# Where a batch's loads stand among the DMA transposes: k and v apart from q, tied in between the u transposes

## The chip, the cores and the metric

The kernel runs on one core of one Trainium2 chip. The metric is the device time of one execution in microseconds (us). PE is TensorE (PEld its weight loads), DVE is VectorE, ACT is ScalarE, POOL is GpSimd, and SP is the queue that issues plain DMA stores and DMA transposes. An *eviction* is a copy of a finished product out of the memory banks that PE writes to; PE can reuse the bank after it. The *granted clock* is the share of full speed at which TensorE was clocked. A kernel's span in its profile is about 2 us shorter than its time.

## The reference, cut to what matters

Linformer attention for 8 batches of 8 heads, then an MLP mixer on each batch:

```python
k_proj = einsum('ks,bhsd->bhkd', E, k)          # k and v: [8, 8, 1024, 64] f32, E and F: [64, 1024]
v_proj = einsum('ks,bhsd->bhkd', F, v)
attn   = softmax(q @ k_proj^T / 8)              # 64 keys
x      = attn @ v_proj                          # heads joined: [8, 1024, 512]
u      = x + (relu(x^T @ w_tok1) @ w_tok2)^T    # token mixing
out    = u + relu(u @ w_ch1) @ w_ch2            # channel mixing
```

## The kernel before

Per batch there is a *front* (k and v projections, scores, attention, token mixing, which yields `u`) and two channel-mixing *half-layers* of 512 rows each. A half-layer needs `u` transposed. SP does this by DMA: `uT0` for the even half-layer, `uT1` for the odd one. I call them the first and the second u transpose. Four additions and subtractions on VectorE, the *S sums*, are the first readers of a uT. While the half-layers of batch b run on PE, the front of batch b+1 is woven in. q is also transposed by DMA. k, v and q are loaded by GpSimd DMAs (f32 to bf16), two of half the heads for each.

The order of every engine's instructions is made before anything runs. A planner in the program gives each job a time, by priority and by the model below, and the instructions are then written down in the order of those times. Each engine's queue then keeps that order on the chip. Semaphores give the waits.

```python
LAG = {"PE": 0.25, "DVE": 0.15, "ACT": 0.15, "POOL": 0.2, "DMA": 1.0}
# every job: engine, occupancy, latency; an engine takes its jobs one after another.
# "DMA" is one such engine, for all loads, stores and transposes together.
def sp(t, fn, **kw):                 # store: t = 1.5, transpose: t = 3.5
    return pl.add("DMA", t, t + 1.0, fn, **kw)

def ld(mb, fn, **kw):                # a load of half the heads: mb = 0.262 * 4
    t = mb / 0.40
    return pl.add("DMA", t, t + 2.0, fn, **kw)

def tie(j, other):                   # j waits for other, in the plan and by a semaphore
    j.deps.add(other)
    tied[j] = other
...
def token2(b, si, due):              # u rows; after the 4th and the 8th: a u transpose
    ...
            if landed[0]:
                tie(j, landed[0])    # the u transpose behind the last-listed load
            turned[0] = j
...
def s_sums(j):                       # half-layer j
    one(0, a21, a22, add=True)       # VectorE, bf16, quarters of uT
    one(2, a11, a21)
    one(1, St[:, 0], a11, deps=(0,))
    one(3, a12, St[:, 1], deps=(1,))
...
def load_batch(b):                   # called in front(b - 1), behind attention
    jobs = [load_heads(b, n, hh, H // 2, None) for n in "kvq" for hh in range(0, H, H // 2)]
    for j in jobs if turned[0] else ():
        tie(j, turned[0])            # behind the second q transpose
    landed[0] = jobs[-1]
...
for b in range(B):
    for j in (2 * b, 2 * b + 1):
        s_sums(j)
        for m in range(SETS):
            up_set(j, m)             # PE: L801 before, L802 after
        down_block(j)                # PE: L896 before, L897 after
    if b + 1 < B:
        at = 2 * TU * (b + 1)
        if b > 0:
            q_transpose(None)
        front(b + 1, at - 62, at - 14)
```

The softmax here doesn't subtract the row's maximum and nothing guards it: scores larger than these inputs give would overflow.

Of the kernel before, what the change touches and what calls it, by code (L numbers as in the profile page):

```python
# [34 lines left out]
class Planner:  # L35
# [36 lines left out]
    def plan(self):  # L72
        for j in self.jobs:
            for d in j.deps:
                d.next.append(j)
        for j in reversed(self.jobs):
            if j.prio is None:
                due = [s.prio for s in j.next]
                j.prio = (min(due) if due else 1e9) - j.occ - 0.3
        for j in self.jobs:  # L80
            if j.prio > 1e8:
                j.prio = max((d.prio for d in j.deps), default=0) + 2
        free = {}
        waiting = {j.n: len(j.deps) for j in self.jobs}
        can = {}
        est = {}

        def open_(j):
            est[j.n] = max((d.end + self.LAG[d.eng] if d.eng != j.eng else d.full for d in j.deps), default=0.0)
            can.setdefault(j.eng, []).append(j)  # L90

        for j in self.jobs:
            if not waiting[j.n]:
                open_(j)
        bank_free = [0.0] * 8
        clean = [True] * 8
        held = dict.fromkeys(self.caps, 0)
        left = {}
        for j in self.jobs:
            for b in j.banks:  # L100
                left[id(b)] = left.get(id(b), 0) + 1
        order = []
        turn = {n: [b for j in self.jobs for b in j.takes if b.stream == n] for n in self.caps}

        def home(b, now):

            if held[b.stream] == self.caps[b.stream]:
                return None
            if b.stream in "UD" and turn[b.stream][0] is not b:
                return None  # L110
            best = None
            keep = [i for i in self.homes["U"] if clean[i] and bank_free[i] is not None]
            if all(clean[:5]):
                keep = []
            for i in self.homes[b.stream]:
                t = bank_free[i]
                if t is None or (b.seeded and not clean[i]):
                    continue
                if not b.seeded and clean[i] and keep and keep[-1] == keep[0] == i:
                    continue  # L120
                c = (max(now, t), clean[i], t, i)
                if best is None or c < best:
                    best = c
            return best

        while any(can.values()):
            pick = None
            for e, js in can.items():
                f = free.get(e, 0.0)
                cands = []  # L130
                for j in js:
                    t = max(f, est[j.n])
                    spot = None
                    if j.takes:
                        h = home(j.takes[0], t)
                        if h is None:
                            continue
                        t, spot = h[0], h[3]
                    cands.append((t, j.prio, j.n, j, spot))
                if not cands:  # L140
                    continue
                t0 = min(c[0] for c in cands) + 0.02
                c = min((c for c in cands if c[0] <= t0), key=lambda c: (c[1], c[2]))
                if pick is None or c[0] < pick[0]:
                    pick = c
            if pick is None:
                raise RuntimeError("no job can go on", [(j.eng, j.fn.__qualname__, j.prio) for js in can.values() for j in js][:20], held, bank_free)
            t, _, _, j, spot = pick
            can[j.eng].remove(j)
            j.start, j.end, j.full = t, t + j.lat, t + j.lat + 0.03  # L150
            free[j.eng] = t + j.occ
            if j.takes:
                b = j.takes[0]
                b.at = spot
                turn[b.stream].remove(b)
                held[b.stream] += 1
                bank_free[spot] = None
            for b in j.banks:
                left[id(b)] -= 1
                if not left[id(b)]:  # L160
                    held[b.stream] -= 1
                    bank_free[b.at] = max(x.end for x in b.jobs) + 0.1
                    clean[b.at] = b.full
            order.append(j)
            for s in j.next:
                waiting[s.n] -= 1
                if not waiting[s.n]:
                    open_(s)
        assert len(order) == len(self.jobs), (len(order), len(self.jobs))
        return order  # L170
# [3 lines left out]
def kernel(  # L174
# [16 lines left out]
    B, H, S, D = q.shape  # L191
# [20 lines left out]
    last = {}  # L212
# [92 lines left out]
    def sp(t, fn, **kw):  # L305
        return pl.add("DMA", t, t + 1.0, fn, **kw)
# [201 lines left out]
            writes=[("kT", 1, h) for h in heads], uses=[bk],  # L508
        )

    turned = [None]
    landed = [None]

    def q_transpose(due):
        for h in range(0, H, H // 2):
            before = turned[0]
            turned[0] = sp(
                3.5,
                lambda h=h: nc.sync.dma_start_transpose(
                    out=qT[:, h : h + H // 2].rearrange("p h j s -> p (h j) s"),  # L520
                    in_=q_sb[:, h : h + H // 2].rearrange("p h si d -> p (h si d)"),
                ),
                reads=[("q", i) for i in range(h, h + H // 2)],
                writes=[("qT", i) for i in range(h, h + H // 2)], prio=due,
            )
            if before:
                turned[0].deps.add(before)

    def q_transpose_pe(hp, due):
        bk = Bank(stream[0], full=False)  # L530
# [93 lines left out]
    def token2(b, si, due):  # L624
        bk = Bank(stream[0], full=False)

        def mm():
            for t in range(TC):
                nc.tensor.matmul(  # L629
                    bank(bk), wt2_sb[:, t, si::NSI], hT_sb[:, t, :],  # L630
                    start=(t == 0), stop=(t == TC - 1),
                )

        pe(
            TC, 512, mm, reads=["wt2"] + [("hT", t, hp) for t in range(TC) for hp in range(HP)],
            takes=[bk], prio=due,
        )
        dve(
            512,
            lambda: nc.vector.tensor_add(  # L640
                out=u_t[b % 2][:, si, :], in0=bank(bk), in1=x_sb[:, si, :]
            ),
            reads=[("x", h, si // NJ) for h in range(H)], writes=[("u", b % 2, si)], uses=[bk],
        )
        if si % NJ == NJ - 1:
            i = si // NJ
            j = sp(
                3.5,
                lambda: nc.sync.dma_start_transpose(
                    out=uT_t[i].rearrange("p s dc q -> p (s dc) q"),  # L650
                    in_=u_t[b % 2][:, i * NJ : (i + 1) * NJ].rearrange("p s d -> p (s d)"),
                ),
                reads=[("u", b % 2, n) for n in range(i * NJ, (i + 1) * NJ)],
                writes=[("uT", i, n) for n in range(HP)], prio=None,
            )
            if landed[0]:
                tie(j, landed[0])
            turned[0] = j

    def quarter(j, sh, dh):  # L660
        return uT_t[j % 2][:, 2 * sh : 2 * sh + 2, 2 * dh : 2 * dh + 2, :]
# [314 lines left out]
            u_transpose_pe(hp, i, (-5.5 if i == 0 else 1.5) + 0.5 * hp)  # L976
    stream[0] = "F"

    def load_batch(b):
        jobs = [load_heads(b, n, hh, H // 2, None) for n in "kvq" for hh in range(0, H, H // 2)]  # L980
        for j in jobs if turned[0] else ():
            tie(j, turned[0])
        landed[0] = jobs[-1]

    def front(b, begin, end):
        units = []
# [5 lines left out]
        for i in range(H // hn):  # L992
            unit(1.9 * hn / H, lambda t, i=i: kv_proj(b, i * hn, hn, t))
            unit(0.9 * hn / H, lambda t, i=i: k_transpose(i * hn, hn, t))
            if b == 1:
                for hp in range(2 * i, 2 * i + 2):
                    unit(0.4, lambda t, hp=hp: q_transpose_pe(hp, t))
        unit(0.4, lambda t: scores(0, t))
        unit(0.4, lambda t: scores(1, t))
        for h in range(H):  # L1000
            if h + 2 < H:
                unit(0.4, lambda t, h=h: scores(h + 2, t))
            for half in range(2):
                unit(0.25, lambda t, h=h, half=half: attend(h, half, t))
        if b + 1 < B:
            unit(0.0, lambda t: load_batch(b + 1))
        for n in range(TC):
            unit(1.8, lambda t, n=n: token1(n, t))
        for si in range(NSI):
# [10 lines left out]
# [4 lines that stand above are left out]
                up_set(j, m)  # L1024
            down_block(j)
        if b + 1 < B:
            at = 2 * TU * (b + 1)
            if b > 0:
                q_transpose(None)
            front(b + 1, at - 62, at - 14)  # L1030
    gate = mybir.DependencyInfo(mybir.DependencyClass.Sync, mybir.DependencyReason.DATA)
    plan = pl.plan()
# [41 lines left out]
```

## Time and profile before

| | before |
|---|---|
| time, median of the first 3 runs | 439.78 us (438.99 to 440.23) |
| PE busy | 418.5 of 439.5 us |
| VectorE waits for a u transpose, before the S sums | 1.5 us, once |
| u transpose, issue to landing | 4.3 to 7.2 us |

The page of the kernel before: its span, the busy times, the granted TensorE clock in 40 slices, and the chain of work that ended last by engine.

```profile
span 439.5 us, 9315 instructions
...
PE 418.5 (95%) x3736; PEld 338.4 (77%) x3736; DVE 321.0 (73%) x783; ACT 241.1 (55%) x439; POOL 106.2 (24%) x122
...
PEclk9999999999999999999999999999999999999999
...
PE 86%; DVE 7%; ACT 2%; DMA 2%; issue 1%; DVEq 0%; ACTq 0%
```

PE is busy nearly always and heads the chain, so a change to loads can only remove the few gaps that PE has. The waits of the kernel before (us in total, how often, the longest):

```profile
PE ps L896 <- DVE da L943: 2.7, 4, 0.9
...
DVE S L671 <- DMA uT<-u: 1.5, 1, 1.5
...
PE ps L578 <- DVE x_sb L595: 0.6, 1, 0.6
```

VectorE stood in front of an S sum once, and PE waited 0.6 us for attention's evictions (`x_sb`). Now the DMA side. First GpSimd's timeline around the loads of batch 4 (start, us, engine, line, operation, in brackets the idle time before it), then SP's around one slow u transpose, then the landing times of all transposes of that tile:

```profile
149.56 0.78 POOL L314 DMA_DIRECT2D q_sb<-in_q_dram  x1 [1.68 <-DMA qT<-q_sb]
...
154.40 1.52 POOL L314 DMA_DIRECT2D k_sb<-in_k_dram  x2
155.90 1.50 POOL L314 DMA_DIRECT2D v_sb<-in_v_dram  x2
157.36 0.78 POOL L314 DMA_DIRECT2D q_sb<-in_q_dram  x1
```

```profile
269.21 4.67 SPq L649 DMA_TRANSPOSE uT<-u  x1
...
287.62 3.09 SPq L649 DMA_TRANSPOSE uT<-u  x1
```

```profile
DMA to landing us min/median/max: 4.3/4.6/7.2
```

The loads go out in one bundle behind the q transposes and are in flight until about the next first u transpose, which beside them took up to 7.2 us (4.3 us for batch 3, when they had all but landed). From batch 2 on, the second u transpose starts 12 to 18 us after the first, when PE has read the old uT.

### The profile page before, as it was taken

How to read it: one execution, taken by the hardware profiler on the slowest of the kernel's cores; microseconds unless marked ns; L12 is line 12 of the kernel's file. 1: busy time of each engine (PE TensorE's matmuls, PEld its weight loads, DVE VectorE, ACT ScalarE, POOL GpSimd, SP SyncE). 2: the span in 40 equal slices, each digit the busy share in tenths (PEclk: the TensorE clock that was granted, in tenths of full speed). 3: DMA queues.
4: the chain of work that ended last, by engine and by line, in shares of the span. 5: the costliest groups of instructions: out<-in, count | busy, mean ns of one | idle time of the engine just before them, and what ended most of it. 6: DMA issues, size and time to landing. Idle time of an engine off the chain costs nothing.

```text
span 439.5 us, 9315 instructions
## 1 busy us (share of the span) xinstructions
PE 418.5 (95%) x3736; PEld 338.4 (77%) x3736; DVE 321.0 (73%) x783; ACT 241.1 (55%) x439; POOL 106.2 (24%) x122
## 2 busy tenths in 40 slices
PE   6789999999999999999999999899999999999993
PEld 4468888578778886788778877688768886888883
DVE  3459969678978797779697696778697596966451
ACT  1557786258536754567356654558436663555540
POOL 8442123032301331115021331115112210212212
PEclk9999999999999999999999999999999999999999
DMA  9999979289955899198955899187992811241022
GB/s 167 208 199 207 206 123 195 91 186 167 177 94 152 126 194 172 46 224 149 197 89 120 139 189 203 22 193 140 199 142 47 195 48 49 50 145 61 36 98 95
DMA packets 89516, 60.89 MB, mean 139 GB/s; under 512 B 55681, under 2 KB 84865, under 8 KB 89473
## 3 DMA queue, kind: packets, MB, share of 16 engines
q0 software_dynamic: 30624, 29.36, 42.7%
q1 hardware_dynamic: 58768, 30.68, 29.4%
q8 instruction: 29, 0.48, 0.4%
q10 hardware_dynamic: 80, 0.26, 0.3%
q14 instruction: 15, 0.11, 0.1%
HBM read 59.24 MB, written 16.78 MB: 173 GB/s over the span
## 4 chain that ended last, share of the span: by engine, by line
PE 86%; DVE 7%; ACT 2%; DMA 2%; issue 1%; DVEq 0%; ACTq 0%
PE ps L896 32%; PE ps L801 30%; PE ps L609 6%; PE ps L629 5%; PE ps L555 3%; PE ps L455 3%; PE ps L578 3%; DMA uT<-u 2%; DVE S L671 1%; DVE u L728 1%; PE ps L539 1%; ACT qT L547 1%; PE ps L377 1%; PE ps L689 1%; DVE da L943 1%
## 5 line engine op out<-in xcount | busy, mean ns | idle before, releaser
L896 PEld LDWEIGHTS <-G 128*128 128x128 bf16 x1344 | 130.0, 98 | 24.5 <-issue 5.7
L896 PE MATMUL ps<-wc_sb,G 128*128 128x256 bf16 x768 | 103.8, 273 | 3.9 <-DVE da L943 2.7
L801 PEld LDWEIGHTS <-wc_sb 128*128 128x128 bf16 x768 | 73.6, 98 | 14.3 <-issue 1.6
L823 ACT ACTIVATE G<-ps 128x512 bf16<-128x512 f32 x96 | 57.2, 599 | 39.9 <-PE ps L801 39.6
L896 PE MATMUL ps<-wT,G 128*128 128x256 bf16 x576 | 77.7, 272 | 0.1
L927 POOL TENSOR_TENSOR o<-o,u 128x512 f32<-128x512 f32 x32 | 37.4, 1169 | 130.3 <-ACT o L925 115.2
L801 PEld LDWEIGHTS <-wT 128*128 128x128 bf16 x576 | 55.1, 98 | 11.2 <-issue 2.2
L801 PE MATMUL ps<-uT,wc_sb 128*128 128x256 bf16 x384 | 57.6, 273 | 0.0
L801 PE MATMUL ps<-S,wc_sb 128*128 128x256 bf16 x384 | 57.6, 273 | 0.0
L927 POOL TENSOR_TENSOR db<-db,u 128x512 f32<-128x512 f32 x16 | 18.9, 1182 | 157.5 <-ACT db L925 157.5
L801 PE MATMUL ps<-S,wT 128*128 128x256 bf16 x384 | 54.9, 273 | 0.9 <-ACT G L823 0.7
L640 DVE TENSOR_TENSOR u<-ps,x_sb 128x512 bf16<-128x512 f32 x56 | 35.7, 684 | 22.2 <-PE ps L629 21.7
L595 DVE TENSOR_TENSOR x_sb<-ps,rdn 128x256 bf16<-128x256 f32 x128 | 49.7, 415 | 0.3
L836 DVE TENSOR_TENSOR G<-G 128x512 bf16<-128x512 bf16 x96 | 46.7, 489 | 3.4
L782 DVE CUSTOM_DVE_ANT_0 g<-ps,ub 128x512 bf16<-128x512 f32 x48 | 32.8, 684 | 20.4 <-PE ps L801 20.3
L782 DVE CUSTOM_DVE_ANT_0 G<-ps,ua 128x512 bf16<-128x512 f32 x48 | 32.7, 682 | 18.1 <-ACT ua L829 18.0
L564 ACT ACTIVATE a<-ps 128x512 bf16<-128x512 f32 x64 | 37.1, 600 | 12.4 <-PE ps L555 12.2
L829 ACT COPY ua<-ps 128x512 f32<-128x512 f32 x48 | 28.1, 586 | 24.2 <-PE ps L801 23.6
L829 ACT COPY ub<-ps 128x512 f32<-128x512 f32 x48 | 28.1, 586 | 9.6 <-PE ps L801 9.2
L842 ACT COPY ps<-ps 128x512 f32<-128x512 f32 x48 | 28.3, 589 | 6.9 <-DVE g L782 4.2
L578 PE MATMUL ps<-vb,a 128*128 128x130 bf16 x256 | 30.9, 226 | 0.6 <-DVE x_sb L595 0.6
L629 PE MATMUL ps<-hT_sb,wt_sb 128*128 128x512 bf16 x112 | 29.5, 379 | 0.0
(69 smaller groups left out, 521.7 us busy)
## 6 DMA issues: line engine op xcount, KB each, us to landing
out_dram<-o SPq DMA_DIRECT2D x32, 512.0 KB, 3.6
k_sb<-in_k_dram POOLq DMA_DIRECT2D x14, 512.0 KB, 8.6
v_sb<-in_v_dram POOLq DMA_DIRECT2D x14, 512.0 KB, 13.0
q_sb<-in_q_dram POOLq DMA_DIRECT2D x14, 512.0 KB, 9.9
wc_sb<-in_moe_w_ch_dram POOLq DMA_DIRECT2D x6, 256.0 KB, 12.9
wc_sb<-in_moe_w_ch_dram POOLq DMA_DIRECT2D x4, 384.0 KB, 12.1
k_sb<-in_k_dram POOLq DMA_DIRECT2D x4, 256.0 KB, 6.7
v_sb<-in_v_dram POOLq DMA_DIRECT2D x4, 256.0 KB, 7.2
```

The costliest lines, as they stand in the source:

```text
L564: lambda: nc.scalar.activation(out=a_t[h % 4], in_=bank(bk), func=ACT.Exp, scale=scale),
L578: nc.tensor.matmul(view()[:, 2 * jj : 2 * jj + 2].rearrange("p c d -> p (c d)"), a_t[h % 4][:, j * P : (j + 1) * P], vb[:, h].rearrange("k ...
L595: lambda: nc.vector.tensor_tensor(out=x_sb[:, 4 * half : 4 * half + 4, h * D : (h + 1) * D], in0=view()[:, :, 0:D], in1=rdn[:, :, None].to ...
L629: nc.tensor.matmul(bank(bk), wt2_sb[:, t, si::NSI], hT_sb[:, t, :], start=(t == 0), stop=(t == TC - 1),)
L640: lambda: nc.vector.tensor_add(out=u_t[b % 2][:, si, :], in0=bank(bk), in1=x_sb[:, si, :]),
L782: nc.vector._custom_dve(TENSOR_ADD_SAT, out=out, in0=in0, in1=in1, s0=FMAX, s1=0.0)
L801: nc.tensor.matmul(t[:, c, :], w1_of(n, dd, 2 * m + c), a_of(j, n, dd), start=(n in (1, 7) and c == 0 and dd == 0), stop=(c == 1 and dd == 1),
L823: lambda: nc.scalar.activation(out=G[:, n, cs], in_=view(src), func=ACT.Relu),
L829: 512, lambda: nc.scalar.copy(out=dst, in_=view("y")), writes=[(name, s % 2)],
L836: 512, lambda: f(out=G[:, n, cs], in0=in0, in1=in1), ps=False, reads=deps,
L896: nc.tensor.matmul(view(X_OF[n])[:, t, :], G[:, G_OF[n], cc, t * P : (t + 1) * P], w2_of(n, cc), start=(n in (1, 7) and t == 0 and cc == 0 ...
L927: 512, lambda: nc.gpsimd.tensor_add(out=dst, in0=dst, in1=u_of(sh, dh)),
```

## The change

The intent, as the edit reads: the loads are parted into two groups, and each is tied in between transposes, so that no transpose runs beside loads. k and v of batch b+2 go behind the k and v projections of batch b+1 and behind batch b's first u transpose, and batch b's second u transpose waits for the last of them. The q loads go behind the q transposes, and the next first u transpose waits for them. The q transposes themselves move forward, behind the second u transpose of the batch before the one they followed.

```diff
-                due = [s.prio for s in j.next]
+                due = [s.prio for s in j.next if s.prio is not None]
...
-    def q_transpose(due):
+    def q_transpose(b, behind):
...
+        landed[0] = load_group(b + 1, "q", j) if b + 1 < B else None
...
-            if landed[0]:
+            if i == 0 and landed[0]:
                 tie(j, landed[0])
-            turned[0] = j
+            turned_u[b, i] = j
...
-    def load_batch(b):
-        jobs = [load_heads(b, n, hh, H // 2, None) for n in "kvq" for hh in range(0, H, H // 2)]
-        for j in jobs if turned[0] else ():
-            tie(j, turned[0])
-        landed[0] = jobs[-1]
+    def load_group(b, names, behind):
+        jobs = [load_heads(b, n, hh, H // 2, None) for n in names for hh in range(0, H, H // 2)]
+        for j in jobs if behind else ():
+            tie(j, behind)
+        return jobs[-1]
+
+    def load_kv(b):
+        last = load_group(b, "kv", turned_u.get((b - 2, 0)))
+        if (b - 2, 1) in turned_u:
+            tie(turned_u[b - 2, 1], last)
...
+        if b + 1 < B:
+            unit(0.0, lambda t: load_kv(b + 1))       # in front(b), behind the projections
+        if b == 1:
+            unit(0.0, lambda t: load_group(2, "q", None))
...
-                q_transpose(None)
+                q_transpose(b + 1, turned_u.get((b - 1, 1)))
```

More of the change, by code (lines that the diff above doesn't have):

```diff
@@ L509, in k_transpose @@
         )
-    turned = [None]
+    turned_u = {}
     landed = [None]
-    def q_transpose(due):
+    def q_transpose(b, behind):
         for h in range(0, H, H // 2):
-            before = turned[0]
-            turned[0] = sp(
+            j = sp(
                 3.5,
@@ L523, in q_transpose @@
                 reads=[("q", i) for i in range(h, h + H // 2)],
-                writes=[("qT", i) for i in range(h, h + H // 2)], prio=due,
+                writes=[("qT", i) for i in range(h, h + H // 2)], prio=None,
             )
-            if before:
-                turned[0].deps.add(before)
+            if behind:
+                j.deps.add(behind)
+            behind = j
+        landed[0] = load_group(b + 1, "q", j) if b + 1 < B else None
     def q_transpose_pe(hp, due):
@@ L1004, in front @@
                 unit(0.25, lambda t, h=h, half=half: attend(h, half, t))
-        if b + 1 < B:
-            unit(0.0, lambda t: load_batch(b + 1))
         for n in range(TC):
```

## The prediction

> **What bounds it now.** The page gives PE 418.5 of 439.5 us (95%). The Trainium skill ("Trainium Kernel Development and Optimization", opening section) warns that matmul busy time is a bad metric because matmuls overlap, so I looked at the spacing of starts: 256-column matmuls start 0.109 us apart, and from 40 to 427 us only about 4 us are lost in gaps (0.85 us at 92, 0.71 and 0.61 at 280-283, 0.73 at 327, 0.55 at 358, 0.44 at 381). Over 2% faster (8.8 us) is not to be had.
>
> **What loads cost now.** In the DMA issues, batch b+1's six loads go out after batch b's second q transpose (q, k, k, v, v, q) and run until the u transpose: 149.6 to 174.3, 250 to 274, 300 to 326 us. The u transpose's tie is to the q half issued first, so it runs beside the others. Alone it lands in 4.3 us (173.6); beside loads it took 7.15 (269.2) and 6.54 us (321.0). This agrees with the same skill page ("Key Constraints": all queues share the 16 DMA engines). There the S sums, its readers, start on landing (276.4, 327.9), and the PE gaps at 280 and 327 follow: about 2 us in all. That is what the change can win.
>
> **What it moves.** No arithmetic, no bytes. The two q loads stay behind the q transposes; the four of k and v go between the first and second u transpose. The loads' priority no longer sees the u transpose's due, so I expect issue order k, k, v, v, and the tie on the last v makes the second u transpose wait for all four: the first lands 5.5 us after issue, others 2.55 us apart (landings 44.6 to 57.4): 13.2 us, plus 0.55 us to issue. Now the second u transpose starts 7.6 to 11.3 us after the first landed (held by PE readers of the old uT); so it moves 3 to 6 us later, and the q transposes queue behind it. For batch 1, where both u transposes go at 87 and 90 us, the second slips to about 105, and batch 2's q transposes by about 15 us.
>
> **New loop.** First u transpose (4.3) + k/v loads (13.75) + second u transpose and both q transposes (12.2, from 287.6 to 299.65) + q landing to the next u transpose (20 to 24 now; about 17 if attention is put first) = 47 to 51 us, estimated. PE's period is about 49.3 us. Five such loops follow 91.7 us, then about 103 us of work (estimated from matmul counts times 0.109): 91.7 + 5 x 49.3 + 103 = 441. So the slack in the DMA chain is spent. I expect slightly slower, near break-even.
>
> **Predicted:** 442 us, 80% range 437 to 452. Faster by 2%: 0.02; same: 0.80; slower: 0.18.
>
> **What would show it.** First u transposes all landing in 4.3 to 4.6 us, no loads beside them; second u transposes 13 us or more after that landing; batch 2's scores at about 115 instead of 101 us; the gaps near 280 gone but new ones where S sums wait for uT. PE busy stays about 418 us.
>
> **What would make it wrong.** If attention cannot be compressed below 20 us, the loop takes 51 us or more and the time reaches 450. If the last v is issued first, the second u transpose hardly moves and the time falls to 437-438. The static order of all engines is replanned, which alone can move a microsecond or two.

## The result, and the profile after

The changed kernel took 457.18 us (median of 4 runs, 455.83 to 459.05), the kernel before 440.00 (4 runs, 438.99 to 443.09). The ratio is 1.038 with a 95% interval of 1.032 to 1.045. It is slower by 3.8%, outside the predicted range. Ratios here are the mean time of one kernel's fast runs over that of the other's of the same rounds, so not quite the ratio of the medians that I quote. Executions over 1.5% slower than the fastest of the same kernel are left out of the means.

The page of the changed kernel, the lines that answer to those above:

```profile
span 455.9 us, 9334 instructions
...
PE 421.7 (92%) x3736; PEld 338.5 (74%) x3736; DVE 320.2 (70%) x783; ACT 243.3 (53%) x439; POOL 105.2 (23%) x122
...
PEclk9799999999899999998999999998999999999998
...
PE 78%; DVE 10%; DMA 7%; ACT 2%; issue 1%; DVEq 0%; ACTq 0%
```

Busy times hardly changed (PE +3.2 us), but PE's share of the chain fell from 86 to 78%, and DMA's rose from 2 to 7%. Three dips of the granted clock have appeared inside the kernel. Its waits:

```profile
DVE S L672 <- DMA uT<-u: 16.4, 6, 3.5
...
PE ps L579 <- DVE x_sb L596: 5.5, 5, 2.7
...
PE ps L802 <- DMA uT<-u: 4.6, 2, 3.6
...
PE ps L802 <- DVE x_sb L596: 2.9, 1, 2.9
```

VectorE now stands in front of S sums six times, 16.4 us in all, and PE waits for u transposes and for attention's evictions. In GpSimd's and SP's timelines around the k and v loads of batch 5:

```profile
185.91 1.15 POOL L928 TENSOR_TENSOR o<-o,u 128x512 f32<-128x512 f32 x1 [2.28 <-ACT o L926]
187.35 1.52 POOL L314 DMA_DIRECT2D k_sb<-in_k_dram  x2 [0.29 <-PE ps L458]
188.86 0.76 POOL L314 DMA_DIRECT2D v_sb<-in_v_dram  x1
194.11 1.15 POOL L928 TENSOR_TENSOR o<-o,u 128x512 f32<-128x512 f32 x1 [4.49 <-ACT o L926]
195.22 0.79 POOL L314 DMA_DIRECT2D v_sb<-in_v_dram  x1
```

```profile
177.91 1.98 SPq L650 DMA_TRANSPOSE uT<-u  x1
195.29 1.55 SPq L921 DMA_DIRECT2D out_dram<-o  x2
205.17 1.78 SPq L650 DMA_TRANSPOSE uT<-u  x1
```

The loads start 9.4 us after the first u transpose, because PE (the projection, L458) still reads the buffers. The last v goes out 7.9 us after the first k and lands at 205.12, 17.8 us after it, with two stores in flight beside it. The second u transpose starts at 205.17, which is 27.3 us after the first. In the kernel before, these gaps were 2.9 us for batch 1 and 12.1 to 18.4 us after that. What that does on VectorE and on PE, in their timelines:

```profile
206.29 0.75 DVE L596 TENSOR_TENSOR x_sb<-ps,rdn 128x256 bf16<-128x256 f32 x2
209.57 1.15 DVE L672 TENSOR_TENSOR S<-uT 128x512 bf16<-128x512 bf16 x1 [2.52 <-DMA uT<-u]
...
211.10 0.42 DVE L596 TENSOR_TENSOR x_sb<-ps,rdn 128x256 bf16<-128x256 f32 x1
```

```profile
208.43 0.28 PE L579 MATMUL ps<-vb,a 128*128 128x130 bf16 x2
211.57 1.01 PE L802 MATMUL ps<-uT,wc_sb 128*128 128x256 bf16 x4 [2.87 <-DVE x_sb L596]
```

An S sum stands at the head of VectorE's queue and its operand lands at 209.55. Attention's matmuls were done by 208.7, but the eviction that would free PE's next bank runs only at 211.1, behind the S sum. So PE stands for 2.87 us. The Trainium skill ("TensorE: Matmul & The Clock Gate", section "Architectural detail") says that ACT and DVE are strict FIFO, and this trace agrees. And PE runs at half speed just afterwards. The windows view of the changed kernel (columns: stretch, length, busy time and instructions of each engine, granted clock, DMA share, GB/s):

```profile
207.40:210.80 3.40, 1.31 (x14) 1.09 (x13) 1.23 (x3) 1.64 (x3) 1.18 (x2) 1.00 1.14 212
210.80:214.20 3.40, 2.62 (x13) 1.89 (x13) 2.78 (x10) 1.17 (x2) 0.00 (x0) 0.50 1.02 192
```

There are three such windows (118.6, 210.8 and 316.6 us), each of 3.4 us at half clock behind a PE gap of 2.7 to 3.6 us. They cost at most 3 x 1.7 = 5.1 us (half of each window). They are not the main loss: two other runs of this kernel, with a mean clock of 0.994 instead of 0.978, had room for at most one such window and still took 455.83 and 456.49 us, only 2.0 and 1.4 us less. The landing times of all transposes of that tile in the changed kernel:

```profile
DMA to landing us min/median/max: 4.2/4.5/8.9
```

The transposes did become quick, as intended: the slow one, 8.9 us, is batch 1's first, beside the first q loads.

### The profile page after: what moved, and what is told of

Read it like the earlier page. It is cut to its first block, busy times and chain, and to the rows that moved or that the text cites. A ratio compares the mean times of both kernels' runs of the same rounds, so it can differ in the third digit from the quotient of the medians.

```text
span 455.9 us, 9334 instructions
## 1 busy us (share of the span) xinstructions
PE 421.7 (92%) x3736; PEld 338.5 (74%) x3736; DVE 320.2 (70%) x783; ACT 243.3 (53%) x439; POOL 105.2 (23%) x122
## 4 chain that ended last, share of the span: by engine, by line
PE 78%; DVE 10%; DMA 7%; ACT 2%; issue 1%; DVEq 0%; ACTq 0%
PE ps L802 29%; PE ps L897 28%; DMA uT<-u 7%; PE ps L610 5%; PE ps L630 5%; PE ps L455 3%; PE ps L579 3%; PE ps L556 3%; DVE S L672 2%; DVE x_sb L596 1%; DVE G L837 1%; DVE u L729 1%; ACT qT L548 1%; PE ps L377 1%; PE ps L540 1%
## 5 line engine op out<-in xcount | busy, mean ns | idle before, releaser
L897 PEld LDWEIGHTS <-G 128*128 128x128 bf16 x1344 | 131.0, 98 | 27.8 <-issue 4.0
L897 PE MATMUL ps<-wc_sb,G 128*128 128x256 bf16 x768 | 104.9, 275 | 2.8 <-DVE da L944 1.6
L802 PE MATMUL ps<-uT,wc_sb 128*128 128x256 bf16 x384 | 58.8, 277 | 7.4 <-DMA uT<-u 4.6
L802 PE MATMUL ps<-S,wc_sb 128*128 128x256 bf16 x384 | 58.6, 276 | 0.0
L802 PE MATMUL ps<-S,wT 128*128 128x256 bf16 x384 | 56.5, 276 | 0.6 <-DVE S L672 0.6
L928 POOL TENSOR_TENSOR db<-db,u 128x512 f32<-128x512 f32 x16 | 18.4, 1152 | 158.6 <-ACT db L926 158.6
L596 DVE TENSOR_TENSOR x_sb<-ps,rdn 128x256 bf16<-128x256 f32 x128 | 50.8, 415 | 0.7
L641 DVE TENSOR_TENSOR u<-ps,x_sb 128x512 bf16<-128x512 f32 x56 | 38.0, 686 | 12.6 <-PE ps L630 12.3
L837 DVE TENSOR_TENSOR G<-G 128x512 bf16<-128x512 bf16 x96 | 43.7, 460 | 3.6 <-DVE G L837 0.5
L783 DVE CUSTOM_DVE_ANT_0 G<-ps,ua 128x512 bf16<-128x512 f32 x48 | 32.8, 684 | 15.8 <-ACT ua L830 15.2
L830 ACT COPY ua<-ps 128x512 f32<-128x512 f32 x48 | 28.1, 586 | 22.4 <-PE ps L802 21.8
L579 PE MATMUL ps<-vb,a 128*128 128x130 bf16 x256 | 31.7, 224 | 5.8 <-DVE x_sb L596 5.5
L830 ACT COPY ub<-ps 128x512 f32<-128x512 f32 x48 | 28.1, 586 | 14.6 <-PE ps L802 14.6
L843 ACT COPY ps<-ps 128x512 f32<-128x512 f32 x48 | 27.9, 580 | 14.9 <-PE ps L802 13.6
L630 PE MATMUL ps<-hT_sb,wt_sb 128*128 128x512 bf16 x112 | 32.7, 381 | 0.0
```

Of the source, the lines that this page charges most:

```text
L579: nc.tensor.matmul(view()[:, 2 * jj : 2 * jj + 2].rearrange("p c d -> p (c d)"), a_t[h % 4][:, j * P : (j + 1) * P], vb[:, h].rearrange("k ...
L596: lambda: nc.vector.tensor_tensor(out=x_sb[:, 4 * half : 4 * half + 4, h * D : (h + 1) * D], in0=view()[:, :, 0:D], in1=rdn[:, :, None].to ...
L630: nc.tensor.matmul(bank(bk), wt2_sb[:, t, si::NSI], hT_sb[:, t, :], start=(t == 0), stop=(t == TC - 1),)
L641: lambda: nc.vector.tensor_add(out=u_t[b % 2][:, si, :], in0=bank(bk), in1=x_sb[:, si, :]),
L783: nc.vector._custom_dve(TENSOR_ADD_SAT, out=out, in0=in0, in1=in1, s0=FMAX, s1=0.0)
L802: nc.tensor.matmul(t[:, c, :], w1_of(n, dd, 2 * m + c), a_of(j, n, dd), start=(n in (1, 7) and c == 0 and dd == 0), stop=(c == 1 and dd == 1),
```

## The experiments

*Waits* below is the total of VectorE's waits for a u transpose before S sums, over the whole span. *Last v* is the time from the first issue to the landing of the last of batch 5's four loads. *uT1* is the time from the start of batch 3's first u transpose to the landing of its second. Times are medians of the fast runs; waits, last v and uT1 are from one profiled run each. Ratio is against the kernel before in the same rounds. The row of the kernel before gives its first three runs. Its medians in the three later sessions were 439.8 to 440.1 us.

| kernel | time, us | ratio (95%) | waits | last v | uT1 |
|---|---|---|---|---|---|
| before | 439.8 | 1 | 1.5 | (other place) | 17.7 |
| changed | 457.2 | 1.038 (1.032 to 1.045) | 16.4 | 17.8 | 31.6 |
| e1_no_wait | 449.3 | 1.020 (1.013 to 1.028) | 9.8 | 18.4 | 30.5 |
| e2_burst | 457.1 | 1.039 (1.034 to 1.044) | 16.3 | 18.1 | 32.0 |
| e3_untied | 452.5 | 1.028 (1.024 to 1.032) | 13.0 | 14.3 | 24.4 |
| e4_first | 458.4 | 1.040 (1.033 to 1.046) | 16.7 | 15.8 | 27.8 |
| e5_small_stores | 459.0 | 1.043 (1.037 to 1.049) | 17.6 | 17.7 | 31.6 |
| e6_small_loads | 440.2 | 1.003 (0.999 to 1.006) | 1.6 | 13.3 | 28.1 |
| e7_honest_plan | 440.0 | 1.001 (0.999 to 1.004) | 4.2 | 17.8 | 31.7 |
| e8_early_kv | 454.3 | 1.033 (1.027 to 1.038) | 8.8 | 14.4 | 26.2 |
| e9_small_stores_all | 446.6 | 1.015 (1.011 to 1.018) | 7.6 | 15.6 | 29.5 |
| e10_sums_later | 453.0 | 1.030 (1.026 to 1.035) | 13.0 | 17.4 | 31.3 |
| e11_plan_half | 442.8 | 1.006 (1.003 to 1.009) | 7.4 | 16.8 | 30.7 |
| e12_best | 437.4 | 0.994 (0.991 to 0.996) | 2.0 | 17.8 | 31.8 |

### First round: is it the wait?

My first theory (A) was that the semaphore wait of the second u transpose on the last v costs the time. Rivals: the replanned order as such (B), and competition on the DMA engines (C). In e1 every engine's order is exactly that of the changed kernel (compared instruction by instruction), and only the wait is gone.

```diff
-            tie(turned_u[b - 2, 1], last)
+            turned_u[b - 2, 1].deps.add(last)        # e1: in the plan only
```

> The changed kernel with every engine's instruction order exactly as it was; only the second u transpose no longer waits on the chip for the last v load (the planner still believes in it). Theory A (the wait costs the time: the second u transpose starts 27 us after the first instead of 22.6 us as planned, and the odd half-layer's products wait for it): 436 to 442 us, second u transposes start within 1 us after their old buffer is free, PE gaps of 2 to 3.6 us before the products gone. Theory B (the replanned order of the engines costs it): stays at 452 us or more. Theory C (loads and transposes now compete for the DMA engines): stays above 450 us, with u transposes that take over 6 us.

Half of the loss came back, not all, and the interval is wide. SP's timeline and the transposes' landing times show why:

```profile
193.57 7.61 SPq L650 DMA_TRANSPOSE uT<-u  x1
```

```profile
DMA to landing us min/median/max: 4.2/6.6/14.9
```

Without the wait the transpose starts earlier and runs beside two loads and two stores. It landed at 205.04, 30.5 us after the first u transpose had started, almost as late as before (31.6). Theory A in its simple form falls: with the wait or without it, uT1 lands when the loads have landed. Theory C's slow transposes did come (10.0 to 14.9 us for the second ones of batches 1 to 5), and the time is just under its 450 us. From the start of its first transpose, uT1 landed 0.8 to 2.4 us earlier than in the changed kernel in batches 1 to 5, 7.4 us in all, about the 7.9 us that came back.

e2 issues the four loads back to back (it moves them together in the plan's list when the planner is done). The order of the other engines is unchanged.

```diff
+    for jobs in bursts:                              # the four k and v loads of a batch
+        at = min(plan.index(j) for j in jobs)
+        rest = sorted(jobs, key=plan.index)
+        for j in rest:
+            plan.remove(j)
+        plan[at:at] = rest
```

> The changed kernel, with the four k and v loads of a batch issued back to back on the GpSimd queue, so that the last v no longer stands behind an addition that waits for ScalarE (in the changed kernel it is issued 7.9 us after the first load). The tie stays. Theory A, second half (the 4 to 5 us by which the chip is later than the plan come from that issue): last v lands 13 to 14 us after the first issue instead of 18, second u transpose starts 4 to 5 us earlier per batch, and the time falls by most of the 17 us, to 439 to 446 us. If the stores' traffic delays the loads, not the late issue: last v still lands 17 us or more after the first issue and the time stays above 452 us.

A clean miss. The last v was issued 2.2 us after the first k instead of 7.9 us, and it landed after 18.1 us all the same. With these stores in flight, issuing it earlier does not make it land earlier.

e3 takes the tie out of the plan as well; e4 ties the second u transpose to the first k load instead of the last v.

```diff
-        if (b - 2, 1) in turned_u:                   # e3
-            tie(turned_u[b - 2, 1], last)
...
-        return jobs[-1]                              # e4
+        return jobs[0] if names == "kv" else jobs[-1]
```

> The changed kernel without the tie between the last v load and the second u transpose, in the plan too (so the order is replanned). Theory A: 436 to 442 us, as without the wait alone; the rest of the change (k and v two batches ahead, q behind its transposes) then costs nothing and may win the 2 us of the u transposes that ran beside loads. Theory B: like the changed kernel, over 450 us, unless the order itself was made bad by the tie.

> The second u transpose is tied to the first k load of the four, not to the last v. The first k load lands 5.5 us after its issue, so 14.5 us after the first u transpose's start plus the 4.7 us that the k buffer's readers take: second u transposes start about 15 us after the first ones instead of 27. Theory A: 437 to 443 us. Theory C (competition): the transposes run beside three loads and take over 6 us, and the time stays above 448 us.

Both missed. uT1 did land earlier relative to uT0 (24.4 and 27.8 us instead of 31.6), and yet e3 gained little and e4 nothing. So lateness counted from the first transpose does not order the times. VectorE's waits do (13.0 and 16.7 us). In e3 and e4 the planner, too, believed in an earlier uT1 and put the S sums earlier: from the first S sum of an even half-layer to that of the odd one, VectorE's queue advances 47 or 48 places in the changed kernel (batches 1 to 5), 40 or fewer in e3 and e4, and 53 to 61 in e7 below.

### Second round: late by the clock, or later than planned?

That gave theory D: what costs is that uT1 lands later *than the order was planned for*. The planner gives four loads in a row 3 x 2.62 + 2.62 + 2.0 = 12.5 us (its `ld`), and it models all DMA as one queue in which a store waits for its turn. On the chip the four took 16.7 to 20.6 us in the changed kernel. Two forms: D1, only the mismatch costs; D2, the lateness itself starves PE in any order. e7 tells these apart: it tells the planner alone.

```diff
-    def ld(mb, fn, **kw):
+    def ld(mb, fn, late=0.0, **kw):
         t = mb / 0.40
-        return pl.add("DMA", t, t + 2.0, fn, **kw)
+        return pl.add("DMA", t, t + 2.0 + late, fn, **kw)
...
+            late=5.0 if b > 2 and name in "kv" else 0.0,
```

> The changed kernel; the planner alone is told that the k and v loads of batches 3 to 7 land 5 us later, as they do on the chip. Nothing else changes; the order of the engines is replanned with the S sums later in VectorE's queue. Theory D1 (only the mismatch between plan and chip costs): VectorE's waits before S sums fall below 3 us between 170 and 345 us and the time falls to 440 to 447 us although the second u transpose starts as late as before. Theory D2 (the lateness itself starves PE, whatever the order): 452 us or more.

440.0 us, the whole loss recovered, with uT1 as late as ever (31.7 us after the first transpose's start; 31.6 in the changed kernel). D2 falls. In the waits view of e7, and in its timelines of SP and of VectorE for the same batch:

```profile
DVE S L673 <- DMA uT<-u: 4.2, 2, 2.4
```

```profile
171.10 3.29 SPq L651 DMA_TRANSPOSE uT<-u  x1
...
198.39 1.79 SPq L651 DMA_TRANSPOSE uT<-u  x1
```

```profile
202.59 0.72 DVE L597 TENSOR_TENSOR x_sb<-ps,rdn 128x256 bf16<-128x256 f32 x2
203.23 0.69 DVE L673 TENSOR_TENSOR S<-uT 128x512 bf16<-128x512 bf16 x1
```

The second transpose lands at 202.78, and attention's evictions now stand in front of the S sum, which finds its operand there. No gap.

e6 tests the same from the other side: the changed kernel's own order (identical on PE, VectorE, ScalarE and SP; on GpSimd only the loads' sizes differ), but loads that are not late. Its output is wrong, which doesn't matter for the time.

```diff
+        few = slice(h, h + 1) if b > 2 and name in "kv" else hs
...
-            dma(dst[:, hs], src[b, hs].rearrange("h (p si) d -> p h si d", p=P)),
+            dma(dst[:, few], src[b, few].rearrange("h (p si) d -> p h si d", p=P)),
```

> Wrong result on purpose. The changed kernel, order and waits untouched; each k or v load of batches 3 to 7 brings one head instead of four. Theory D: the last v, still issued 7.9 us after the first, lands about 12 us after it, the second u transpose starts 6 us earlier per batch, the VectorE waits before the S sums vanish, time 438 to 443 us, what the plan intended. Theory B (the planned order itself is slow on the chip): stays above 450 us.

440.2 us, and the waits are 1.6 us. So the planned order is good if the loads come when it expects them. Theory B falls with this. e6 alone leaves one thing mixed, for it takes away DMA traffic as well as lateness; e7 has all the traffic and is as fast.

e5 asked where the lateness comes from, by shrinking stores (wrong result).

```diff
+        wide = DM // 8 if j % 2 and 1 < j < 12 else DM     # e5; in e9 without "j % 2 and"
...
-                1.5, lambda: nc.sync.dma_start(out=out_v[b, :, rows, :], in_=o_t[os[sh]]),
+                1.5, lambda: nc.sync.dma_start(out=out_v[b, :, rows, :wide], in_=o_t[os[sh]][:, :, :wide]),
```

> Wrong result on purpose. The changed kernel, order and waits untouched; the two stores of each odd half-layer from 3 to 11, which run beside the k and v loads, write 64 of 512 columns. Theory D (the loads end late because stores share the DMA engines with them, so the second u transpose and with it VectorE's S sums come later than the order was planned for): last v lands 13 to 14 us after the first issue instead of 18, VectorE's waits before the S sums fall from 8.5 us between 170 and 345 us to under 2, time 440 to 447 us. If stores do not matter: 455 us or more.

This experiment missed its aim: I had shrunk the wrong stores. The two beside the loads (197.9 and 199.1 us) were whole, so nothing changed, and it says nothing about stores. e9 shrank them all:

> Wrong result on purpose. The first try with small stores shrank the pair of stores that did not run beside the loads (their small ones are at 215 and 228 us, those beside the loads at 198 and 199 us were whole). Here all stores of half-layers 2 to 11 write 64 of 512 columns. If the stores delay the last v: it lands 13 to 14 us after the first issue instead of 18, VectorE's waits before the S sums fall from 16 us in all to under 6, time 440 to 448 us. If not: 455 us or more, and the late landing has another cause.

The last v landed after 15.6 us instead of 17.8, the waits fell from 16.4 to 7.6 us and the time to 446.6. So the stores in flight beside the loads are a large part of the lateness, though not all of it: 15.6 is still 3 us more than the planner's 12.5. In e9 the last v still went out 7.9 us after the first k and took 7.7 us, so its late issue may make up that rest; e2's burst with small stores, which would tell, was not run.

e8 let the k and v projections of batches 3 on come 10 us earlier, so that the loads find their buffers free.

```diff
-            unit(1.9 * hn / H, lambda t, i=i: kv_proj(b, i * hn, hn, t))
+            unit(1.9 * hn / H, lambda t, i=i: kv_proj(b, i * hn, hn, t - (10 if b > 2 else 0)))
```

> The changed kernel with the k and v projections of batches 3 on due 10 us earlier, before the token products of the batch before, so that the k and v buffers are free when the first u transpose lands (now 4.8 us later). Theory D: the loads begin about 4 us earlier, meet the stores less, and the second u transpose starts 4 to 8 us earlier relative to the first; time 442 to 450 us. If PE lateness is not from there: 455 us or more.

The loads did begin 5.2 us after the first u transpose's start instead of 9.4 (batch 5's), and the last v landed 14.4 us after the first issue. The waits fell to 8.8 us, but the time only to 454.3, the one run that does not fit the waits. Here the loads' issue, with GpSimd's additions among them, falls onto the S sums of the even half-layer. VectorE's and GpSimd's timelines of e8:

```profile
238.24 2.02 DVE L672 TENSOR_TENSOR S<-uT 128x512 bf16<-128x512 bf16 x2
240.18 0.41 DVE L672 TENSOR_TENSOR S<-S,uT 128x512 bf16<-128x512 bf16 x1
240.63 1.28 DVE L672 TENSOR_TENSOR S<-uT,S 128x512 bf16<-128x512 bf16 x1
```

```profile
238.46 1.17 POOL L928 TENSOR_TENSOR db<-db,u 128x512 f32<-128x512 f32 x1
...
240.48 1.15 POOL L928 TENSOR_TENSOR o<-o,u 128x512 f32<-128x512 f32 x1
```

An S sum takes 0.41 us alone. The two that overlap a GpSimd addition took 1.69 us (the first of the pair, from the trace) and 1.28 us. The Trainium skill ("GPSIMD Engine Reference", section "Specifications") says that GpSimd's SBUF interfaces are shared with VectorE and contend with DVE instructions that have two SBUF inputs, as the S sums have. This trace agrees. It is 2.2 us of VectorE for that batch, and PE pays for it: it stands until VectorE, behind the slow S sums, has made the next G.

```profile
242.57 0.60 PE L802 MATMUL ps<-uT,wT 128*128 128x256 bf16 x4 [1.70 <-DVE G L783]
```

The same happens in three batches of e8, with PE gaps of 2.25 (at 132 us), 1.70 and 1.70 us (at 241 and 293), 5.65 us in all. So e8 swapped one cost for another; that this is all of its excess was not tested.

### Third round: dose, the one queue, and a better kernel

e10 moved only the odd half-layers' S sums, in VectorE's queue alone (the other four queues are identical to the changed kernel's).

```diff
+    for s in [j for j in plan if j in sums]:         # S sums of odd half-layers
+        n = plan.index(s)
+        m = n + 1
+        while s not in plan[m].deps and plan[m].start < s.start + 5.0:
+            m += 1
+        plan.insert(m - 1, plan.pop(n))
```

> The changed kernel with one thing moved: in VectorE's queue alone the four S sums of each odd half-layer stand up to 5 us (by the plan) later, behind other VectorE work; the order on PE, ScalarE, GpSimd and the DMA queues and all waits are as in the changed kernel. Theory D1 (VectorE's queue stands still in front of an S sum whose u transpose has not landed, and attention's evictions behind it starve PE): the waits before S sums fall from 16 us to under 7, time 440 to 446 us. If PE's own order is what loses (its products of the odd half-layer wait for uT too): above 450 us.

It gained 4 us (453.0), not 11 or more. The waits fell only to 13.0 us, so the move was too small to clear them: the first S sum of each four, where the queue stands, came only 0 to 2 places later in VectorE's queue, since the edit stops in front of the next job that depends on the sum; the others moved by up to 14 places. And PE still waited 5.3 us for uT itself (between 95 and 345 us). VectorE's order alone thus carries a part of it. How the rest divides between VectorE's and PE's orders stays open, since e7 changed both.

e11 is e7 with `late=2.5`.

> As the honest plan, but the planner is told 2.5 us of lateness instead of 5. Theory D1: in between, 444 to 452 us, with about half of the VectorE waits before S sums; a step rather than a slope would mean that one order was merely unlucky.

442.8 us and 7.4 us of waits, in between the changed kernel (0 us told, 457.2) and e7 (5 us told, 440.0), though nearer to e7 and a little under the expected 444. That speaks against one lucky order; one point in between does not give the shape of the slope.

e12 is e7 with `late=7.0`, and with the first q loads of the main part behind batch 1's second u transpose:

```diff
-        landed[0] = load_group(b + 1, "q", j) if b + 1 < B else None
+        behind = turned_u[1, 1] if b == 2 else j
+        landed[0] = load_group(b + 1, "q", behind) if b + 1 < B else None
```

> The honest plan with 7 us of lateness, and the first q loads of the main part moved behind batch 1's second u transpose, so that batch 1's first u transpose (9 us beside them, 4.3 alone) runs alone. Theory D1: the waits before S sums at 95 and 154 us go, 435.5 to 439 us, 0.5 to 1% faster than the kernel before; if the front of the kernel is bound otherwise, 440 us as the honest plan.

437.35 us (6 runs, 436.71 to 438.33), against 440.06 of the kernel before (11 runs): ratio 0.994, interval 0.991 to 0.996. It beats both kernels by a clear, small margin. Batch 1's first u transpose landed in 4.2 us instead of 8.9. Lines of the page and of the waits view of e12:

```profile
span 436.1 us, 9296 instructions
...
PEclk9599999999999999999999999999999999999999
```

```profile
DVE S L674 <- DMA uT<-u: 2.0, 2, 1.1
```

The clock no longer dips inside the kernel (nor does it in e7), and with the plan corrected the change is a little over half a per cent faster than the kernel before. Which of e12's two additions won the 2.6 us over e7 was not tested apart.

## Why the prediction was wrong

- **"Over 2% faster is not to be had", "about 2 us in all".** Right. The best version that I found wins 2.7 us, and PE stood still for only 5.6 us between 40 and 430 us before (390 us less 384.4 us busy).
- **"New ones where S sums wait for uT".** Right: those are the waits of 16.4 us. **"Slightly slower".** The direction was right, but by luck: the reason given, a DMA chain with no slack left, is not what cost the time (below).
- **"PE busy stays about 418 us"; first u transposes clean.** Right in the main: 421.7 us, part of it at half clock, and most transposes landed in 4.2 to 5.1 us. But batch 1's first took 8.9 us and batch 2's 5.9 us beside q loads, and the largest second transpose was 5.0 us.
- **"Issue order k, k, v, v, and the tie on the last v makes the second u transpose wait for all four".** Right: 205.12 and 205.17 us.
- **"13.2 us, plus 0.55 us to issue".** Mis-sized. From the landing of the first u transpose (182.52) to the second's start (205.17) it took 22.65 us: 4.8 us until the projection had left the k buffers, and 17.8 us for the loads, where the issue order and the stores had been left out. I had taken the spacing of landings from a stretch where no stores ran. So batch 3's second u transpose started 27.3 us after the first instead of 12.6 before, 14.6 us later and not 3 to 6.
- **"New loop".** This model was wrong, not only its sizes. I read the q transposes as those of the batch whose attention follows. They are one batch ahead: batch 4's ran at 156 to 164 us and its scores began at 193. So they are not in the loop that I drew. Batch 2's scores began at 90 us, not 115, earlier than before (101). The first u transposes of batches 2 to 6 did come 51.9 to 54.0 us apart, which looks like the feared loop of 51 us or more; but in e7, with the same waits on the chip, the last three of these four distances are 49.5 to 49.6 us.
- **"The static order of all engines is replanned, which alone can move a microsecond or two".** This is the step that failed. I treated the planned order as noise and the DMA chain as the bound. The runs show the reverse: with uT1 equally late, 457.2 and 440.0 us differ by nothing but what the planner was told (e7), and the changed order with loads on time takes 440.2 (e6). The loss is the difference between plan and chip: six waits of VectorE, 16.4 us in all, against a loss of 17.2 us. The numbers lie close, but a wait of VectorE is not worth its own length exactly. PE's own account is more direct: between 40 and 430 us it stood still for 17.3 us (390 less 372.7 busy) instead of 5.6, and the half-clock windows cost up to 5.1 us: 16.8 us together, where the profiled span grew by 16.4. In e7 PE stood still for 7.0 us. There the DMA chain that I had feared does not bind: from batch 3 to 5 each first u transpose starts within 0.03 us of the end of the last `u` row, the q loads having landed 1.0 to 1.5 us before.

What stays open: the part of the loads' lateness that is not stores, the split of the loss between VectorE's and PE's order, and whether the slow S sums are all of e8's excess.

## What to carry to other kernels

An order that is fixed before the run is only as good as the durations it was planned with: when a change puts a DMA in front of an instruction at the head of an in-order queue, compare when the plan expects the landing with when the trace shows it, and correct the plan before judging the change. A transfer that was slack in the old schedule may have had a wrong duration all along without any cost. To tell "too late" from "later than planned", change only what the planner is told, and leave every transfer and every wait of the program as it is.

## What the Trainium skill lacked or had wrong

- "TensorE: Matmul & The Clock Gate" ("Why this matters for your kernels") advises no PE-idle gaps over about 3 us and speaks of one idle window. In the changed kernel PE gaps of 2.87 and 2.66 us were each followed by 3.4 us at clock 0.50, and in the 3.4 us just ahead of the first of these two slow stretches PE was busy for 1.31 us, so that stretch was not idle. So a gap under 3 us can be followed by half clock here. The length of one gap does not decide it: gaps of 2.02 and 1.92 us in the same run, and one of 2.70 us in e5, were not followed by such a stretch, and one of 2.25 us in e8 was.
- "DMA: Bandwidth & Descriptors" ("Rules for kernel authors") says that a transpose next to ordinary DMAs needs nothing. The results stayed correct, but no page says what it costs: a u transpose took 4.3 us alone and 10.0 to 14.9 us beside k and v loads and stores (second transposes of batches 1 to 5 in e1).
- No page has the mismatch between an order fixed beforehand and the chip's DMA times as a cause of loss. Here it was worth 17 us of 457.
